# Smaller VectorE operations in the fold, and the last batch's routing gathered into one run

## The chip, the cores and the metric

One core of a Trainium2 chip runs one program. The metric is device time in microseconds (us), the median of three runs of the same kernel. The engines are TensorE (PE; its weight loads are PEld), VectorE (DVE), ScalarE (ACT), GpSimd (POOL) and SyncE (SP, which only issues DMAs here). Each takes its instructions from one queue, in order.

## The reference

The input `x` is 8 batches of 1856 rows of 256 floats. The reference takes the real part of the 2D Fourier transform of each batch and feeds the 14,848 resulting rows to a two-level mixture of experts:

```
X = fft(fft(x, axis=1), axis=2).real
group  = argmax of 4 group logits;  expert = argmax of that group's 4 expert logits
out[row] = softmax weight of group * softmax weight of expert * (relu(row @ w1[expert]) @ w2[expert])
```

There are 16 experts; `w1` is 256x1024 and `w2` is 1024x256 for each.

## The kernel before

**Phase 1** is the transform, batch by batch. `fold` (L414) adds and subtracts mirrored quarters of the batch on VectorE (`fold_rows`, `quarters`, `columns`), in place in the tiles `xq` and `BD`, and splits the result into a high and a low float16 half, `ghl` (`hi_half` on ScalarE, `lo_half` on VectorE). `s_stage` multiplies by the cosine and sine tables (matmuls `pu`, results in `U`), `leftovers` collects the odd columns in `Um`, `d_stage` does the second transform and the router's logits (matmuls `pr` and `pl`, 8 tiles for an odd batch), `rows` copies `pr` to row tiles, and `route` (L680) turns the logits into an expert, a place and a weight for each row: some twenty short VectorE steps in a chain, from the copy `lg` of `pl` to the places `posi`. It ends with 14 or 15 scatters on GpSimd that write the rows to their expert's region of a DRAM buffer, `XS`.

All work of phase 1 goes through wrappers (`self.V`, `self.A`, `self.M`, `self.Q`) that pin an instruction behind the one written just before it on its engine. Its order is written by hand: in a string such as ORDER7 each letter advances one generator by a step (F fold, S s_stage, D d_stage, L leftovers, R route, W weights, X first rows) or takes one postponed piece (s, I, i, l, d, t).

**Phase 2** is the experts. A *job* is up to four tiles of 128 rows of one expert: `layer1` (8 groups of 6 matmuls into `ph`, then ScalarE and VectorE write the halves of `hT`), and one job later `layer2` (24 matmuls into `py` for each tile, a ScalarE copy to `y`, a scatter of `y` to the output). PSUM has four buffers for `ph` (and `pu`) and two for `py` (and `pr`); `y` has four. Jobs 0, 1 and 2 take rows of which the places were settled early (after batches 4 and 6; `early_load`); jobs 3, 4 and 5 finish the same three experts and, like all that follow, need every routed row: their rows are gathered from `XS` on GpSimd with places that exist only when the last batch is routed. Then each of the other 13 experts has two jobs (4 and 3 tiles), with overflow jobs of one tile between them; job 6 is the first overflow job.

`turn_steps` (L1075) prepares a job's rows: cast to high and low halves `xh`, and a DMA transpose to `xT`. `split_steps` (L1022) prepares one expert's weights (a *unit*; units 0, 1 and 2 belong to the first three experts, unit 3 to the first overflow slot, unit 4 to the fourth expert): four square sums on ScalarE (`junk`), a small matmul, then four pairs of ScalarE and VectorE operations from the staging tile `wst` to `whl`. Units share one staging tile (overflow slots have their own).

Where instructions are not pinned (all of `layer1` and `layer2`, `turn_steps` in jobs from 2 on) a planner orders each engine's queue before the run: of the instructions that its own model of time takes as ready, the one written first. `tick` (L1288) is called after each step of a layer. It advances `weights` by about one step for each 1000 ns of planned TensorE work, the next job's row preparation by a step, and `tail`, which runs the last batch's rest, ORDER8, up to its next `|`. The routing must be complete before the first gathers are written, so `fetch(3)`, at the start of job 1, runs whatever is left of the tail. Before, ORDER8 has 30 bars: the eight ticks of job 0 write its first five products, unit 1's whole weight split comes next, and then the other products and all of the routing.

Of the kernel before, what the change touches and what calls it, by code (L numbers as in the profile page):

```python
# [14 lines left out]
ALU = mybir.AluOpType  # L15
# [23 lines left out]
WPART = 1024  # L39
LPARTS = 4  # L40
LASTZ = 7

RATE, T1, T2 = 1000, 320, 2570

# [8 lines left out]
ORDER5 = 'RsFLdFZsDlZIdsSdSZFSlFRSLLRDsDFSRRlZNZldDsdLIRSIUDLNRFSIUNRNdiDdlsUZstdDRsUZ'  # L53
ORDER6 = 'sRIDZFdISLstdSLFSssslNZiLRNZNFDRNdFRlZDSDFRSRLIdSDRRLSNUdidLsIRNRlUssDFtdRZs'
ORDER7 = 'IZWSiSZtdDLDDNLZLZZdDFldWsDdNDRDILRURRRRWSdIdRSRsRWLXSSiIZXSRlsXtUIiiURDRRsWRlSsXWXXRWWXXWSLRRWWXlWWWWWWXWWWWWWW'
ORDER8 = 'I||sisDLD|dDLi||DDsLd|||DDdL||DRRRRR||||||||dRR|IR|DRDRRRRDR|DLRLR|R||||RRdRR||d|RR|R'
BIG = 1.0e6
RS = 2.0 ** -11
E23 = 2.0 ** 23
# [206 lines left out]
class K:  # L266
# [150 lines left out]
    def fold(self, b, x, fp):  # L417

        V, sm, c32 = self.V, self.sm, self.c32
        xa, xc = x  # L420
        flat = lambda t: t.rearrange("p m e n -> p (m e n)")
        acc = sm.tile([P, 2], F32, name="acc")
        pn = self.misc[:, 480 + b:481 + b]
        ei = sm.tile([P, 1], I32, name="x_ei")
        v = sm.tile([P, NV], F32, name="x_v", bufs=4)
        sx = v[:, 0:1]
        e = sm.tile([P, NV], F32, name="x_e")
        def fold_rows(q):
            o = slice(4 * q, 4 * q + 4)
            V.tensor_tensor(out=xa[:, o], in0=xa[:, o], in1=xc[:, o], op=ALU.add)  # L430

        def squares(q):
            junk = self.cp.tile([P, 4 * 257], mybir.dt.bfloat16, name="junk", tag="junk")
            self.A.activation(junk[:, 0:4 * 257], xa[:, 4 * q:4 * q + 4].rearrange("p a d -> p (a d)"),
                              AF.Square, scale=2.0 ** 0.5, accum_out=acc[:, q:q + 1])

        def total():
            for q in range(2):
                self.M.matmul(pn, lhsT=self.one_b, rhs=top(acc)[:, q:q + 1], start=q == 0, stop=False)
            self.M.matmul(pn, lhsT=self.one_b, rhs=top(self.xa4)[:, b:b + 1], start=False, stop=True)  # L440

        def quarters(pm):
            V.tensor_tensor(out=xc[:, 4 * pm:4 * pm + 4], in0=xa[:, 0:4], in1=xa[:, 4:8],
                            op=(ALU.add, ALU.subtract)[pm])

        def columns(eo, m0, m1):
            t = xc[:, 4 * m0:4 * m1].rearrange("p (m c) d -> p m c d", c=4)
            V.tensor_tensor(out=BD[:, m0:m1, eo].rearrange("p m (c d) -> p m c d", d=128),
                            in0=t[:, :, :, eo:eo + 128], in1=t[:, :, :, 256 - eo:128 - eo:-1],
                            op=(ALU.add, ALU.subtract)[eo])  # L450

        def lo_half(part):
            V.scalar_tensor_tensor(out=part(hl[:, 1]), in0=part(BD), scalar=sx, in1=part(hl[:, 0]),
                                   op0=ALU.mult, op1=ALU.subtract)

        def hi_half(part):
            self.A.activation(part(hl[:, 0]), part(BD), AF.Copy, scale=sx)

        def exponent():
            V.tensor_scalar(out=ei, in0=pn.bitcast(I32), scalar1=24, scalar2=None,  # L460
                            op0=ALU.logical_shift_right)

        def exponents():
            V.tensor_tensor(out=e, in0=ei.broadcast_to([P, NV]), in1=c32[:, C_MUL:C_MUL + NV], op=ALU.mult)

        def powers():
            V.tensor_tensor(out=v.bitcast(I32), in0=e, in1=self.addv[:, b], op=ALU.add)

        for q in range(2):
            fold_rows(q)  # L470
            squares(q)
            yield
        if b == 0:
            BD = fp.tile([P, 2, 2, 512], F32, name="BD")
            hl = fp.tile([P, 2, 2, 2, 512], F16, name="ghl", bufs=2)
            self.fds[b] = hl, v
            total()
            quarters(0)
            columns(0, 0, 1)
            V.tensor_scalar(out=ei, in0=pn.bitcast(I32), scalar1=24, scalar2=None,  # L480
                            op0=ALU.logical_shift_right)
            V.tensor_scalar(out=sx.bitcast(I32), in0=ei, scalar1=-E23, scalar2=199 * E23, op0=ALU.mult,
                            op1=ALU.add)
            hi_half(lambda t: t[:, 0, 0])
            quarters(1)
            columns(0, 1, 2)
            hi_half(lambda t: t[:, 1, 0])
            yield
            columns(1, 0, 2)
            lo_half(lambda t: t[:, :, 0])  # L490
            yield
            hi_half(lambda t: t[:, :, 1])
            yield
            exponents()
            V.tensor_tensor(out=v[:, 1:].bitcast(I32), in0=e[:, 1:], in1=self.addv[:, b, 1:], op=ALU.add)
            lo_half(lambda t: t[:, :, 1])
            yield
            return
        total()
        yield  # L500
        for pm in range(2):
            quarters(pm)
            yield
        self.now("l")
        BD = fp.tile([P, 2, 2, 512], F32, name="BD")
        hl = fp.tile([P, 2, 2, 2, 512], F16, name="ghl", bufs=2)
        self.fds[b] = hl, v
        for eo in range(2):
            columns(eo, 0, 2)
            yield  # L510
        exponent()
        yield
        exponents()
        yield
        powers()
        yield
        hi_half(flat)
        for pm in range(1, -1, -1):
            self.later("l", lambda pm=pm: lo_half(lambda t: t[:, pm].rearrange("p e n -> p (e n)")))
        yield  # L520

    def later(self, letter, f):
# [638 lines left out]
    def phase2(self, wp):  # L1161
        tc, nc = self.tc, self.nc
        wpa = self.wpa
        with tc.tile_pool(name="h", bufs=2, reuse_waits="tile") as hp, \
# [4 lines left out]
            units, jobs = [], []  # L1169
# [5 lines left out]
            first = earliest()  # L1175
# [7 lines left out]
            o = 0  # L1183
            for e in range(len(first), NE):
# [3 lines left out]
                u = unit("s", e)  # L1188
# [14 lines left out]
            free = lambda u: -1 if before[u] is None else last[before[u]]  # L1203
            todo = sorted(range(1, len(units)), key=lambda u: (max(free(u), 0), u))
            st, ready, infos, xs = {}, {0: self.w0}, {}, {}
            state = dict(split=None, done=-1, t=0, tail=self.last_rows())

            def tail():
                if state["tail"]:
# [13 lines left out]
            def loads():  # L1223
                for u in todo:
                    if u not in st and all(pools(v)[0] != pools(u)[0] for v in st) and pools(u)[0] in pool \
                            and (units[u][0] == "s" or infos):
                        load(u)

            def weights():

                if state["split"] is None:
                    if not todo or free(todo[0]) > state["done"] or (units[todo[0]][0] == "o" and not infos):
                        return False
                    loads()
                    pn = self.misc[:, 490 + 2 * todo[0]:492 + 2 * todo[0]] if state["tail"] else self.ps.tile([P, 2], F32, name="pn", tag="misc")
                    state["split"] = self.split_steps(pool[pools(todo[0])[1]], st[todo[0]],
                                                      self.V, self.A, nc.tensor, pn, 2)
                try:
                    next(state["split"])
                except StopIteration as e:  # L1240
                    u = todo.pop(0)
                    ready[u], state["split"] = e.value, None
                    del st[u]
                    loads()
                return True
# [18 lines left out]
            def prep(n):  # L1264
                if n < len(jobs):
                    xs[n] = self.x0[n] if n < len(self.x0) else \
                        (yield from self.turn_steps(qp, *xs[n], nc.vector, nc.scalar, nc.sync))

            def tick(g, t):
                state["t"] += t  # L1270
                while state["t"] >= RATE:
                    state["t"] = state["t"] - RATE if weights() else 0
                next(g, None)
                tail()

            pend = None
            fetch(0)
# [3 lines left out]
            for n, (u, kind, slots) in enumerate(jobs):  # L1281
                while u not in ready:
                    assert weights()
                w, inv = ready[u]
                g = prep(n + 1)
                xT, wt = xs.pop(n)
                cw, toks = self.slot_weights(qp, wt, inv)
                fetch(n + 2)  # L1288
                hT = finish(self.layer1(hp, w, xT, len(slots)), lambda: tick(g, T1 * len(slots)))
                if pend:  # L1290
                    finish(self.layer2(*pend), lambda: tick(g, T2))
                    state["done"] = n - 1
                for _ in g:
                    pass
                pend = (qp, w, hT, cw, toks)
# [52 lines left out]
```

## Time and profile before

| | us |
|---|---|
| median of 3 runs (893.53 to 899.07) | 894.63 |
| the profiled execution | 889.18 |
| its span | 887.2 |
| TensorE busy in the span | 813.2 (92%) |
| VectorE, ScalarE, GpSimd busy | 531.7, 583.9, 393.9 |

Busy time is the sum of the engine's instructions in the profiled execution; a row's idle time is the gap in front of an instruction, with the event that ended it. Phase 1 lasts until about 184 us, the last batch's products and routing until about 250 us, and from there TensorE is busy in nearly all slices to the end.

### The profile page before, as it was taken

To read this page: it belongs to the slowest core of one execution; us is meant where nothing else is said; L and a number is where in the kernel's file an instruction comes from. 1 tells how busy PE (TensorE), PEld (TensorE's weight loads), DVE (VectorE), ACT (ScalarE), POOL (GpSimd) and SP (SyncE) were. 2 spreads that over 40 slices of the span, in tenths; PEclk is the share of its full clock that TensorE was granted. 3 is DMA by queue.
4 is the path that set the end of the run, shared out by engine and by line. 5 is a ranking of instruction groups with operands and counts; after the bars stand their busy time and mean duration, and the time that the engine had idled before them with its cause. 6 is when DMAs were issued, how large, how long until landed. Compare 5 with 4: busy or idle time off the path is not lost.

```text
span 887.2 us, 17624 instructions
## 1 busy us (share of the span) xinstructions
PE 813.2 (92%) x6375; PEld 580.5 (65%) x6375; DVE 531.7 (60%) x1286; ACT 583.9 (66%) x1190; POOL 393.9 (44%) x372
## 2 busy tenths in 40 slices
PE   2788989978968899799999999999999999999997
PEld 1466656635845586658686868686867777776766
DVE  6599788567625456556475665657575656566330
ACT  2576666867445477867587777768786877685331
POOL 1008777773677453515343535353443434332113
PEclk9999999979998999989999999999999999999999
DMA  9925553687287655646665758483839475632101
GB/s 348 336 96 187 193 203 116 205 239 189 70 292 197 114 166 156 181 126 169 153 177 164 194 127 225 112 264 79 273 94 235 130 206 160 175 75 52 40 19 40
DMA packets 110184, 145.86 MB, mean 164 GB/s; under 512 B 76395, under 2 KB 81799, under 8 KB 108304
## 3 DMA queue, kind: packets, MB, share of 16 engines
q1 hardware_dynamic: 92768, 99.96, 39.4%
q0 software_dynamic: 16896, 44.55, 17.0%
q8 instruction: 50, 0.82, 0.4%
q10 hardware_dynamic: 432, 0.22, 0.2%
q14 instruction: 38, 0.31, 0.1%
HBM read 97.18 MB, written 33.29 MB: 147 GB/s over the span
## 4 chain that ended last, share of the span: by engine, by line
PE 50%; issue 11%; DMA 10%; POOL 4%; DVE 3%; ACT 2%; SPq 2%; POOLq 0%; ACTq 0%; DVEq 0%
PE ph L1122 26%; PE py L1138 23%; DMA xT<-xh 6%; POOL XS L790 2%; POOL out L790 2%; DVE whl L244 2%; SPq L1091 1%; DMA wst<-w 1%; ACT whl L244 1%; DMA xg<-XS 1%; DMA xg<-XS,ii_s 1%; DMA XS<-xq,posi 1%; DVE hT L1126 0%; ACT xh L1083 0%; DMA XS<-whl,posi 0%
## 5 line engine op out<-in xcount | busy, mean ns | idle before, releaser
L1122 PE MATMUL ph<-xT,whl 128*128 128x384 f16 (+2 forms) x2112 | 368.2, 320 | 19.1 <-DVE hT L1126 8.8
L1138 PE MATMUL py<-whl,hT 128*128 128x256 f16 x2976 | 370.2, 274 | 13.8 <-ACT y L1143 11.4
L1138 PEld LDWEIGHTS <-hT 128*128 128x128 f16 x2976 | 288.1, 98 | 76.5 <-issue 13.7
L1126 DVE SCALAR_TENSOR_TENSOR hT<-ph,hT 128x128 f16<-128x128 f32 (+2 forms) x352 | 180.7, 529 | 167.2 <-ACT hT L1125 165.9
L1122 PEld LDWEIGHTS <-whl 128*128 128x128 f16 x2112 | 187.1, 99 | 137.1 <-issue 22.0
L790 POOL DMA_INDIRECT out<-y,tok x124 | 135.3, 1092 | 212.7 <-ACT y L1143 143.1
L1125 ACT ACTIVATE hT<-ph 128x128 f16<-128x128 f32 (+2 forms) x352 | 158.9, 471 | 93.3 <-PE ph L1122 90.6
L1069 POOL DMA_INDIRECT xg<-XS,ii_s x100 | 115.0, 1150 | 165.6 <-DVE hT L1126 82.8
L244 DVE SCALAR_TENSOR_TENSOR whl<-wst,e_v,whl 128x1024 f16<-128x1024 f32 x112 | 138.6, 1279 | 20.4 <-ACT whl L244 19.4
L244 ACT ACTIVATE whl<-wst,e_v 128x1024 f16<-128x1024 f32 x112 | 121.8, 1139 | 8.1 <-DVE e_v L244 7.5
L244 ACT ACTIVATE junk<-wst 128x1024 bf16<-128x1024 f32 x112 | 118.2, 1055 | 11.8 <-DMA wst<-w 11.3
L1143 ACT ACTIVATE y<-py,cws 128x256 f32<-128x256 f32 x124 | 58.6, 474 | 74.5 <-PE py L1138 58.9
L244 PE MATMUL pu<-CS,ghl 128*128 128x464 f16 (+3 forms) x384 | 84.4, 371 | 4.4 <-ACT ghl L244 4.4
L1085 DVE TENSOR_TENSOR xh<-xg,xh 128x256 f16<-128x256 f32 x116 | 48.2, 418 | 54.5 <-ACT xh L1083 54.5
L790 POOL DMA_INDIRECT XS<-whl,posi x42 | 46.8, 1115 | 73.6 <-ACT row L244 61.5
L1083 ACT CAST xh<-xg 128x256 f16<-128x256 f32 x116 | 45.1, 402 | 41.4 <-DMA xT<-xh 36.1
L244 PEld LDWEIGHTS <-ghl 128*128 128x128 f16 (+1 forms) x384 | 44.5, 119 | 36.0 <-ACT ghl L244 4.7
L790 POOL DMA_INDIRECT XS<-row,posi x45 | 51.0, 1132 | 13.9 <-issue 12.8
L244 PEld LDWEIGHTS <-U 128*128 128x128 f16 x672 | 43.1, 97 | 17.1 <-issue 9.5
L244 PE MATMUL pr<-c,U 128*128 128x256 f16 x336 | 46.4, 273 | 7.9 <-ACT whl L244 5.2
L244 DVE TENSOR_TENSOR xq<-xq 128x1028 f32<-128x1028 f32 x32 | 38.9, 1220 | 6.4 <-DMA xq<-xq 6.3
L244 ACT CAST U<-pu 128x464 f16<-128x464 f32 (+3 forms) x64 | 33.4, 549 | 12.0 <-PE pu L244 11.7
(151 smaller groups left out, 420.6 us busy)
## 6 DMA issues: line engine op xcount, KB each, us to landing
wst<-w SPq DMA_DIRECT2D x108, 512.0 KB
xq<-xq SPq DMA_DIRECT2D x14, 1028.0 KB
CS<-cs SPq DMA_DIRECT2D x8, 464.5 KB
xq<-xq SPq DMA_DIRECT2D x4, 514.0 KB
wst<-w SPq DMA_DIRECT2D x8, 256.0 KB
xT<-xh SPq DMA_TRANSPOSE x124
out<-y,tok POOLq DMA_INDIRECT x124
xg<-XS,ii_s POOLq DMA_INDIRECT x100
```

What stands on the lines that cost most here:

```text
L244: return self.tc.keep_in_program_order(f(*args, **kw))
L790: ins = self.nc.gpsimd.indirect_dma_start(out=out, out_offset=bass.IndirectOffsetOnAxis(ap=ap, axis=0), in_=in_, in_offset=None, bounds_ch ...
L1069: self.nc.gpsimd.indirect_dma_start(out=xg[:, :].bitcast(I32), out_offset=None, in_=self.XS[:, :], in_offset=bass.IndirectOffsetOnAxis(ap= ...
L1083: A.copy(xh[:, 0], xg[:, 0:D])
L1085: lo = V.tensor_tensor(out=xh[:, 1], in0=xg[:, 0:D], in1=xh[:, 0], op=ALU.subtract)
L1091: Q.dma_start(out=xT[:, :, j * P:(j + 1) * P], in_=xh, transpose=True)
L1122: nc.tensor.matmul(ph[:, 0:n * P], lhsT=w[:, wl, o:o + P], rhs=xT[:, xl * 2 + c, :], start=i == 0, stop=i == 5)
L1125: nc.scalar.activation(hT[:, f, 0], ph[:, 0:n * P], AF.Relu)
L1126: nc.vector.scalar_tensor_tensor(out=hT[:, f, 1], in0=ph[:, 0:n * P], scalar=0.0, in1=hT[:, f, 0], op0=ALU.max, op1=ALU.subtract)
L1138: nc.tensor.matmul(py, lhsT=hT[:, f, hl, j * P:(j + 1) * P], rhs=w[:, wl, 2048 + f * D:2048 + (f + 1) * D], start=i == 0, stop=i == 23)
L1143: nc.scalar.activation(y, py, AF.Copy, scale=cw)
```

## The change

1. The fold's VectorE operations of 1024 or 1028 elements a partition (`fold_rows`, `quarters`, and for batches 1 to 7 `columns` and `lo_half`) become two each, of half the size.
2. ORDER8 keeps four bars. All the products come in its first two parts, the routing in the next three, so the tail is written out by the fifth tick of job 0.
3. In `tick` the tail comes ahead of the next job's row preparation, which waits until the tail is done.
4. Row preparation of early jobs from job 2 on uses the pinned wrappers.
5. Units from 3 on are neither loaded nor split before job 3 (`LATER`, `begun`).

```diff
-ORDER8 = 'I||sisDLD|dDLi||DDsLd|||DDdL||DRRRRR||||||||dRR|IR|DRDRRRRDR|DLRLR|R||||RRdRR||d|RR|R'
+ORDER8 = 'IsisDLDdDLi|DDsLdDDDdLDDDD|dddLLLDDRRRRR|dRRRRRRRRRR|RRRRRRRRRRRRRR'
...
-            o = slice(4 * q, 4 * q + 4)
-            V.tensor_tensor(out=xa[:, o], in0=xa[:, o], in1=xc[:, o], op=ALU.add)
+            for h in range(2):
+                o = slice(4 * q + 2 * h, 4 * q + 2 * h + 2)
+                V.tensor_tensor(out=xa[:, o], in0=xa[:, o], in1=xc[:, o], op=ALU.add)
...
-            columns(eo, 0, 2)
+            for m in range(2):
+                columns(eo, m, m + 1)
...
-            self.later("l", lambda pm=pm: lo_half(lambda t: t[:, pm].rearrange("p e n -> p (e n)")))
+            def low(pm=pm):
+                for eo in range(2):
+                    lo_half(lambda t: t[:, pm, eo])
+            self.later("l", low)
...
+            begun = lambda u: u < len(first) or state["job"] >= LATER
...
-                        (yield from self.turn_steps(qp, *xs[n], nc.vector, nc.scalar, nc.sync))
+                        (yield from self.turn_steps(qp, *xs[n], *((self.V, self.A) if jobs[n][1] == "e" else
+                                                                  (nc.vector, nc.scalar)), nc.sync))
...
-                next(g, None)
                 tail()
+                if not state["tail"]:
+                    next(g, None)
```

`begun(u)` is asked both where `loads` issues a unit's load and where `weights` starts its split; `state["job"]` is set to `n` at the start of job `n`; `LATER` is 3 and `len(first)` is 3. `quarters` is halved as `fold_rows` is.

## Rows read from the trace of the kernel before

**Rows 1.** Stretches: start:end, length, busy PE PEld DVE ACT POOL, granted clock, DMA share, GB/s.
```profile
184.50:271.40 86.90, 76.04 (x543) 51.00 (x544) 45.71 (x139) 49.01 (x100) 53.20 (x52) 0.93 0.66 197
...
254.20:271.40 17.20, 10.85 (x79) 8.56 (x79) 3.13 (x14) 7.99 (x18) 13.24 (x14) 0.80 0.77 237
271.40:317.20 45.80, 38.66 (x269) 26.30 (x268) 24.56 (x67) 25.23 (x55) 24.77 (x24) 0.96 0.68 148
```

**Rows 2.** TensorE in order of time: start, us, what, count, idle before and releaser.
```profile
184.51 2.72 PE L1122 MATMUL ph<-xT,whl 128*128 128x512 f16 x6 [6.24 <-DMA xT<-xh]
...
191.32 0.82 PE L244 MATMUL pr<-c,U 128*128 128x256 f16 x6
...
211.28 0.30 PE L244 MATMUL pl<-RW,Um 128*128 128x20 f16 x6
...
215.26 5.34 PE L1122 MATMUL ph<-xT,whl 128*128 128x512 f16 x24 [3.01 <-DVE hT L1126]
...
235.37 0.19 PE L1038 MATMUL pn<-wacc,one_b 128*128 128x2 bf16 x2
...
254.24 3.22 PE L1138 MATMUL py<-whl,hT 128*128 128x256 f16 x28 [1.53 <-ACT y L1143]
263.77 5.77 PE L1138 MATMUL py<-whl,hT 128*128 128x256 f16 x30 [6.31 <-ACT y L1143]
...
271.39 4.06 PE L1122 MATMUL ph<-xT,whl 128*128 128x384 f16 x24
```

**Rows 3.** ScalarE in order of time, 202 to 262 us.
```profile
202.57 4.25 ACT L244 ACTIVATE whl<-wst,e_v 128x1024 f16<-128x1024 f32 x4
...
210.94 0.90 ACT L1083 CAST xh<-xg 128x256 f16<-128x256 f32 x2 [3.15 <-DMA xg<-XS]
...
216.85 0.49 ACT L244 COPY lg<-pl 128x280 f32<-128x280 f32 x2
...
253.71 0.47 ACT L1143 ACTIVATE y<-py,cws 128x256 f32<-128x256 f32 x1 [2.97 <-DMA out<-y,tok]
...
257.95 1.06 ACT L244 ACTIVATE junk<-wst 128x1024 bf16<-128x1024 f32 x1 [3.28 <-DMA wst<-w]
```

**Rows 4.** Scatters and gathers on GpSimd, 205 to 257 us.
```profile
206.18 0.97 POOL L790 DMA_INDIRECT XS<-xq,posi  x1 [0.31 <-issue]
...
229.15 0.97 POOL L790 DMA_INDIRECT XS<-xq,posi  x1 [0.92 <-issue]
...
249.67 0.97 POOL L790 DMA_INDIRECT XS<-xq,posi  x1 [0.30 <-issue]
...
256.06 1.05 POOL L1069 DMA_INDIRECT xg<-XS,ii_s  x1 [0.30 <-issue]
```

**Rows 5.** VectorE in order of time: unit 1's split and the last batch's places.
```profile
203.74 4.89 DVE L244 SCALAR_TENSOR_TENSOR whl<-wst,e_v,whl 128x1024 f16<-128x1024 f32 x4 [0.35 <-ACT whl L244]
...
227.02 0.56 DVE L244 TENSOR_REDUCE posi<-offp 128x15 int32<-128x240 f32 x1
```

**Rows 6.** SyncE's weight loads, 210 to 243 us.
```profile
210.72 1.79 SPq L1019 DMA_DIRECT2D wst<-w  x4
...
242.14 13.79 SPq L1019 DMA_DIRECT2D wst<-w  x8
```

**Rows 7.** Four VectorE operations of 512; all operations of the fold's last step.
```profile
214.52 2.48 DVE L1126 SCALAR_TENSOR_TENSOR hT<-ph,hT 128x512 f16<-128x512 f32 x4
...
L244 DVE TENSOR_TENSOR BD<-xq x17: 692/1218/1273, 13.3 to 150.3; 128x1024 f32<-128x1024 f32 x15, 128x512 f32<-128x512 f32 x2
```

**Rows 8.** A scatter beside a fold operation; all scatters; the wait for the first early rows.
```profile
108.00 2.38 DVE L244 TENSOR_TENSOR BD<-xq 128x1024 f32<-128x1024 f32 x2
109.26 1.96 POOL L790 DMA_INDIRECT XS<-whl,posi  x1 [0.30 <-issue]
...
L790 POOL DMA_INDIRECT XS<-row,posi x45 | 51.0, 1132 | 13.9 <-issue 12.8
...
172.95 0.40 ACT L244 CAST xh<-xg 128x256 f16<-128x256 f32 x1 [0.31 <-DMA xg<-XS]
```

More of the change, by code (lines that the diff above doesn't have):

```diff
@@ L41 @@
 LASTZ = 7
+LATER = 3
 RATE, T1, T2 = 1000, 320, 2570
@@ L55 @@
 ORDER7 = 'IZWSiSZtdDLDDNLZLZZdDFldWsDdNDRDILRURRRRWSdIdRSRsRWLXSSiIZXSRlsXtUIiiURDRRsWRlSsXWXXRWWXXWSLRRWWXlWWWWWWXWWWWWWW'
-ORDER8 = 'I||sisDLD|dDLi||DDsLd|||DDdL||DRRRRR||||||||dRR|IR|DRDRRRRDR|DLRLR|R||||RRdRR||d|RR|R'
+ORDER8 = 'IsisDLDdDLi|DDsLdDDdLDDDD|dddLLLDDRRRRR|dRRRRRRRRRR|RRRRRRRRRRRRRR'
 BIG = 1.0e6
@@ L442, in quarters @@
         def quarters(pm):
-            V.tensor_tensor(out=xc[:, 4 * pm:4 * pm + 4], in0=xa[:, 0:4], in1=xa[:, 4:8],
-                            op=(ALU.add, ALU.subtract)[pm])
+            for h in (0, 2):
+                V.tensor_tensor(out=xc[:, 4 * pm + h:4 * pm + h + 2], in0=xa[:, h:h + 2],
+                                in1=xa[:, 4 + h:6 + h], op=(ALU.add, ALU.subtract)[pm])
         def columns(eo, m0, m1):
@@ L1205, in phase2 @@
             st, ready, infos, xs = {}, {0: self.w0}, {}, {}
-            state = dict(split=None, done=-1, t=0, tail=self.last_rows())
+            state = dict(split=None, done=-1, t=0, tail=self.last_rows(), job=0)
+            begun = lambda u: u < len(first) or state["job"] >= LATER
             def tail():
@@ L1225, in loads @@
                     if u not in st and all(pools(v)[0] != pools(u)[0] for v in st) and pools(u)[0] in pool \
-                            and (units[u][0] == "s" or infos):
+                            and (units[u][0] == "s" or infos) and begun(u):
                         load(u)
@@ L1231, in weights @@
                 if state["split"] is None:
-                    if not todo or free(todo[0]) > state["done"] or (units[todo[0]][0] == "o" and not infos):
+                    if not todo or free(todo[0]) > state["done"] or (units[todo[0]][0] == "o" and not infos) \
+                            or not begun(todo[0]):
                         return False
@@ L1284, in phase2 @@
                 w, inv = ready[u]
+                state["job"] = n
                 g = prep(n + 1)
```

## The prediction

> **What bounds it now.** I read the stretches first [rows 1], then TensorE in order of time where it idles [rows 2], then each idle's releaser on its own engine [rows 3 to 6]. From 317 us on TensorE is busy in nearly every slice of the page, so time won or lost before that comes out at the end one for one. The place that the change touches lies between job 0's first matmul at 184.51 and job 3's first at 271.39. In its 86.9 us TensorE is busy 76.04 [rows 1]; the missing 10.86 are three gaps of 3.01, 1.53 and 6.31 [rows 2].
>
> Their causes differ. The first gap waits for `hT`, because ScalarE stood 3.15 us at job 2's casts: the planner had put them ahead, and their rows had not landed [rows 3]. The second waits for `y`: a `y` buffer was not free for 2.97 us, as its output scatter stood on GpSimd behind the last batch's fifteen scatters [rows 3, 4]. In the third ScalarE waits at unit 3's square sums, 3.28 us in the first, for a load that SyncE issued over 13.79 us from 242.14 on [rows 3, 6]; a finished `py` waits behind them. [...]
>
> **The change, part by part.** The sum is made against the profiled execution, 889.18 us; the median of the runs is 5.45 higher, and I add that.
>
> *Casts of job 2 pinned, behind the routing.* Four casts, four subtractions and four transposes (on SyncE) move. Their rows need batch 6's scatters, which end at 207.15 [rows 4]; pinned behind job 1's first `hT` (about 216, below) they find them landed. Gap one goes: 3.01. Job 2 starts twenty microseconds later still, so nothing new waits.
>
> *Units from 3 on wait for job 3.* Eight loads and the square sums leave the stretch. Gap three, 6.31, loses its cause, and with it the slow matmuls: 5.77 less 30 x 3.22/28 = 3.45 gives 2.3. Unit 3 is wanted by job 6 alone, over 40 us after job 3's start; its eighteen steps at about 1 us fit. Its work is covered by ScalarE's 20 us of idle in the 45.8 after 271.4 [rows 1]; without that cover it costs its four `whl` operations, 4.25 by the like row of unit 1 [rows 3]. SyncE loses its 13.79 us block, so job 3's transposes can't stand behind it.
>
> *Products and routing in one run.* Now the products run from 191.32 to 211.58 [rows 2] and the routing from the copy at 216.85 to the places at 227.58 [rows 3, 5], 10.73 us. Compact, eight products of about 1 us (0.82 and 0.31 overlapping) [rows 2] with two groups of job 0 between them end near 200; the routing, if it takes its 10.73 again, ends near 211. Batch 6 leaves GpSimd at 207.15, so the fifteen scatters run from about 211 in place of 229.15; they took 21.5 us [rows 4], so they end near 232 and not at 250.64. The gathers come 5.4 after that, near 238, and by the 15.3 us from the first gather to job 3's first matmul [rows 2, 4] rows are ready at 253. TensorE, with its gaps gone, is there at 261: they are not what is late next.
>
> What is moved past: the output scatters of job 0, some of which stood ahead of the fifteen, now queue behind them on GpSimd. Four `y` buffers hold job 0; job 1's first `y` needs one back, about 2.5 us after the fifteen end, so at 234 or 235. TensorE gets there, with its two `py` buffers full, at 231.6: job 0's second layer ends at 216 (184.5, and 2.7 for the first group, 8.3 for products, 9.6 for seven more groups, 10.9 for 96 `py`), job 1's first layer takes 10.6 (eight groups of 1.33 [rows 2]) and two tiles 5. That wait costs between nothing (if unit 2 is ready and job 2 goes first) and 6.31 plus 2.3, the like gap; by these two times it is 3, and I take 3.
>
> Unit 1's four pairs (202.57 to 208.63 [rows 3, 5]) now come behind the routing, from 211 to 218. Job 1 needs half of them, at 215; job 0's second layer, 205 to 216, hides that. Without this cover job 1 stands for up to 10. Unit 2's load is issued when unit 1 leaves the staging tile, at 218 in place of 210.72 [rows 6]. Before, unit 2 was done 31.4 after its load, at 242.1, but its small matmul stood until 235.37 [rows 2] behind the overflow lists, which follow the routing and share its PSUM bank; with the lists done by 217 about 11 of that go, and unit 2 is ready near 238, enough of it at 235, the same time as the first `y`. It is inside the 3.
>
> *Halves.* Sixty VectorE instructions more: four in batch 0, eight in each of seven. Four operations of 1024 in a row take 4.89 us [rows 5], four of 512 take 2.48 [rows 7]: behind one another halves cost nothing. Alone, one of 512 takes 692 ns where 1024 takes 1218 [rows 7], so at most 166 ns each, 10.0 in all. Below nothing: a scatter that starts inside a fold pair takes 1.96 us and ends 0.84 after the pair's end [rows 8]; if half of all the excess over 0.97 in the 45 scatters of the row went, that is 3.6. The halves are written one after the other, so the row of four is the nearest: nothing.
>
> [...]
>
> Sum: 3.01 + 1.53 + 6.31 + 2.3 - 3 = 10.15. The execution would take 879.0, the median **884.5**.
>
> **The rivals.** *The gap moves.* The fifteen scatters hold job 0's outputs longer than I think, and TensorE stands 6.31 again, with 2.3 of slow matmuls behind it, at job 1's second layer: gain 13.15 - 8.6 = 4.5, median 890. For it: GpSimd works its queue in order, and the wait is 3 already. Against it: if unit 2 is ready first, job 2's first layer can go ahead.
>
> *More goes.* From 271.4 to 317.2 TensorE idles another 7.14 [rows 1], job 3 to 5 waiting for ScalarE and transposes. With rows at 253 and unit 3 out of the way some of it can vanish: with 4 of it, 880.5; with all, 877. To this belongs a relief of GpSimd in the fold: were its chain of scatters what job 0 waits for, a start up to 3.6 earlier (873.5 with all). Against that part: the first early rows were waited for only 0.31 us [rows 8]. [...]
>
> *Ahead, but not shorter: slower.* The run stands in front of unit 1's split, and of every output. If its twenty VectorE steps still end at 227.6, each pinned behind a step of job 0, unit 1 is done at 234.7 and job 1 starts at 231, where TensorE is out of work at 216: 15, and 2.3 of slow matmuls. The scatters then end at 249 as before, the first `y` comes back at 252, and TensorE is through job 1's first layer and two tiles at 246.6: 5 and 2.3 more. Gaps one and three with their clock, 11.6, still go: 24.6 - 11.6 = 13 slower, 908. It costs from a run that ends later than 215 and passes 1% from 223 on. For it: the chain took 10.73 with VectorE busy half of the time (45.71 of 86.9 [rows 1]), so it is waiting, not work. Against it: its first part starts some fifteen microseconds earlier.
>
> *It does nothing.* The planner floats unpinned work as before (the loads are not pinned), gaps one and three come back in other places, or halves cost their 10.0 and eat the 10.15: 894.
>
> **How the numbers follow.** About 1% (8.9 us) is what a measurement of this kernel can tell. Chances: forecast 0.48, its own range 879 to 888; gap moves 0.16; more goes 0.16; nothing 0.09; slower 0.11. The range leaves out the slower case and the far end of "more": **874 to 896**. Faster (below 885.7): 0.34 of the forecast and "more": 0.50. Within 1%: the forecast's other 0.14, "gap moves" and "nothing": 0.39. Slower: 0.11.
>
> **What would show it.** In the trace after: the copy `lg` near 200 and the places near 211; the first scatter of the last batch right behind batch 6's, the last before 234; no ScalarE wait for `wst` or for early rows between 205 and 262; TensorE's idle from job 0 to job 3 under 5 us and job 3 at 259 to 264; unit 3's square sums inside job 3; fold operations in pairs of about 1.2 us. I am wrong if the places come after 220, if a gap over 5 us stands at a `py` or at job 1's or 2's first `ph`, or if phase 1 (job 0's first matmul, 184.5) moves by more than 2 either way.

## The result, and the profile after

The changed kernel takes 883.06 us (median of 4, 881.16 to 885.79); the kernel before, run beside it, 896.85 (893.53 to 900.67): a ratio of 0.990 [0.986, 0.993]. The profiled executions, 889.18 before and 883.54 after, lie only 5.64 apart, because the one of before was quicker than every timed run of it. What the traces explain is these 5.64. (The kernel that was measured has `DDsLdDDdLDDDD` as the second part of its order, one D fewer than the diff above.)

I cut both traces at the start of VectorE's first operation on `hT` in job 0 and in job 6, the 1st and the 49th of 352, and call what lies between them the transition:

| us | to job 0 | transition | from job 6 on | span |
|---|---|---|---|---|
| before | 188.2 | 134.8 | 564.3 | 887.2 |
| after | 186.3 | 127.6 | 567.9 | 881.7 |
| difference | -1.9 | -7.2 | +3.6 | -5.5 |

Stretches of the changed kernel: from job 0's first matmul to job 6, jobs 3 to 6, jobs 8 and 9 (columns as in [rows 1]):

```profile
182.56:313.80 131.24, 119.21 (x878) 82.43 (x879) 75.73 (x215) 79.98 (x165) 80.85 (x78) 0.96 0.68 186
...
266.00:332.00 66.00, 66.00 (x530) 49.21 (x529) 35.77 (x86) 45.52 (x90) 28.74 (x26) 1.00 0.47 134
...
338.60:371.20 32.60, 25.71 (x210) 19.81 (x208) 17.19 (x39) 24.25 (x46) 15.79 (x14) 0.93 0.70 193
```

and the first and the last of these in the kernel before:

```profile
184.51:323.00 138.49, 120.50 (x874) 82.63 (x875) 75.43 (x216) 80.03 (x166) 81.28 (x78) 0.94 0.66 176
...
348.00:378.60 30.60, 24.34 (x211) 19.13 (x210) 17.21 (x40) 24.11 (x46) 16.76 (x14) 0.99 0.71 210
```

Between job 0's first matmul and job 6 TensorE's idle falls from 17.99 to 12.03, and its busy time by 1.29 at a higher granted clock (0.96 against 0.94): 7.25 in all. In jobs 8 and 9 2.0 come back, of which 1.37 are busy time at a lower clock (0.93 against 0.99). But the saving does not lie where I had put it. TensorE after, against [rows 2]:

```profile
182.56 2.72 PE L1129 MATMUL ph<-xT,whl 128*128 128x512 f16 x6 [6.26 <-DMA xT<-xh]
...
185.47 1.10 PE L245 MATMUL pr<-c,U 128*128 128x256 f16 x6
...
197.44 0.30 PE L245 MATMUL pl<-RW,Um 128*128 128x20 f16 x6
...
212.53 4.48 PE L1129 MATMUL ph<-xT,whl 128*128 128x512 f16 x20
...
235.48 6.82 PE L1145 MATMUL py<-whl,hT 128*128 128x256 f16 x38 [4.89 <-ACT y L1150]
246.08 5.34 PE L1129 MATMUL ph<-xT,whl 128*128 128x512 f16 x24 [3.78 <-issue]
...
255.30 1.45 PE L1129 MATMUL ph<-xT,whl 128*128 128x512 f16 x6 [1.72 <-DVE hT L1133]
...
260.06 1.14 PE L1129 MATMUL ph<-xT,whl 128*128 128x384 f16 x6
```

Job 1 now starts without a gap, but from job 0 to job 3 TensorE still idles 11.15 us (0.29, 0.47, 4.89, 3.78 and 1.72; the first two not shown), where it was 10.86. What has gone is the idle behind job 3: from 266 to 332 TensorE is busy 66.00 of 66, where [rows 1] had 7.14 of idle between 271.4 and 317.2. (From job 3's first matmul to job 6 the idle is 0.67, where it was 7.13.)

The last batch's chain on VectorE, ScalarE and GpSimd, against [rows 3 to 5], a fence each:

```profile
208.91 0.56 DVE L245 TENSOR_REDUCE posi<-offp 128x15 int32<-128x240 f32 x1
...
212.25 1.32 DVE L245 SCALAR_TENSOR_TENSOR whl<-wst,e_v,whl 128x1024 f16<-128x1024 f32 x1
```

```profile
198.53 0.49 ACT L245 COPY lg<-pl 128x280 f32<-128x280 f32 x2
...
221.58 1.06 ACT L245 ACTIVATE junk<-wst 128x1024 bf16<-128x1024 f32 x1 [1.82 <-DMA wst<-w]
...
231.85 3.22 ACT L245 ACTIVATE whl<-wst,e_v 128x1024 f16<-128x1024 f32 x3
...
234.98 0.81 ACT L1150 ACTIVATE y<-py,cws 128x256 f32<-128x256 f32 x2
242.79 0.40 ACT L1090 CAST xh<-xg 128x256 f16<-128x256 f32 x1 [7.00 <-DMA xg<-XS,ii_s]
```

```profile
211.04 0.97 POOL L797 DMA_INDIRECT XS<-xq,posi  x1 [2.62 <-issue]
...
230.22 0.97 POOL L797 DMA_INDIRECT XS<-xq,posi  x1 [0.30 <-issue]
231.49 0.97 POOL L797 DMA_INDIRECT out<-y,tok  x1 [0.30 <-issue]
...
234.59 2.09 POOL L1076 DMA_INDIRECT xg<-XS,ii_s  x1 [0.78 <-DVE whl L245]
```

Against [rows 6], SyncE's issues: unit 2's four loads at 217.40, then the eight of units 3 and 4 among job 2's and job 3's transposes:

```profile
217.40 1.82 SPq L1026 DMA_DIRECT2D wst<-w  x4
223.54 8.15 SPq L1098 DMA_TRANSPOSE xT<-xh  x3
234.03 2.01 SPq L1026 DMA_DIRECT2D wst<-w  x4
236.73 1.53 SPq L1098 DMA_TRANSPOSE xT<-xh  x1
238.36 1.04 SPq L1026 DMA_DIRECT2D wst<-w  x2
243.69 5.55 SPq L1098 DMA_TRANSPOSE xT<-xh  x3
249.29 1.26 SPq L1026 DMA_DIRECT2D wst<-w  x2
```

The scatters' means and the fold's last step, against [rows 7, 8]:

```profile
L797 POOL DMA_INDIRECT XS<-row,posi x45 | 50.2, 1116 | 13.9 <-issue 11.6 <-ACT whl L245 0.6 <-ACT U L245 0.5
L797 POOL DMA_INDIRECT XS<-whl,posi x42 | 44.9, 1070 | 74.2 <-ACT row L245 61.9 <-issue 11.6 <-DVE m L245 0.3
...
L245 DVE TENSOR_TENSOR BD<-xq x31: 668/684/1218, 13.0 to 149.3; 128x512 f32<-128x512 f32 x30, 128x1024 f32<-128x1024 f32 x1
```

### The profile page after: what moved, and what is told of

It reads as the page before. It is cut to its first block, busy times and chain, and to the rows that moved or that the text cites. A ratio compares the mean times of both kernels' runs of the same rounds, so it can differ in the third digit from the quotient of the medians.

```text
span 881.7 us, 17685 instructions
## 1 busy us (share of the span) xinstructions
PE 814.3 (92%) x6375; PEld 581.4 (66%) x6375; DVE 536.2 (61%) x1346; ACT 583.8 (66%) x1190; POOL 390.1 (44%) x372
## 3 DMA queue, kind: packets, MB, share of 16 engines
q0 software_dynamic: 16896, 44.55, 17.9%
## 4 chain that ended last, share of the span: by engine, by line
PE 37%; issue 7%; DMA 5%; POOL 2%; ACT 1%; DVE 1%; SPq 0%; POOLq 0%; ACTq 0%
PE ph L1129 19%; PE py L1145 18%; DMA xT<-xh 5%; POOL out L797 2%; SPq L1098 0%; DVE whl L245 0%; DVE hT L1133 0%; ACT junk L245 0%; ACT xh L1090 0%; SPq L1026 0%; DVE xh L1092 0%; ACT whl L245 0%; ACT y L1150 0%; POOLq L797 0%; ACT hT L1132 0%
## 5 line engine op out<-in xcount | busy, mean ns | idle before, releaser
L1129 PEld LDWEIGHTS <-whl 128*128 128x128 f16 x2112 | 186.3, 99 | 134.1 <-issue 17.8
L797 POOL DMA_INDIRECT out<-y,tok x124 | 132.6, 1070 | 209.8 <-ACT y L1150 140.4
L1076 POOL DMA_INDIRECT xg<-XS,ii_s x100 | 117.4, 1174 | 170.5 <-DVE hT L1133 78.7
L797 POOL DMA_INDIRECT XS<-whl,posi x42 | 44.9, 1070 | 74.2 <-ACT row L245 61.9
L245 DVE TENSOR_TENSOR xq<-xq 128x514 f32<-128x514 f32 x64 | 41.1, 686 | 5.9 <-DMA xq<-xq 5.9
```

The source lines that it names most:

```text
L245: return self.tc.keep_in_program_order(f(*args, **kw))
L797: ins = self.nc.gpsimd.indirect_dma_start(out=out, out_offset=bass.IndirectOffsetOnAxis(ap=ap, axis=0), in_=in_, in_offset=None, bounds_ch ...
L1076: self.nc.gpsimd.indirect_dma_start(out=xg[:, :].bitcast(I32), out_offset=None, in_=self.XS[:, :], in_offset=bass.IndirectOffsetOnAxis(ap= ...
L1129: nc.tensor.matmul(ph[:, 0:n * P], lhsT=w[:, wl, o:o + P], rhs=xT[:, xl * 2 + c, :], start=i == 0, stop=i == 5)
```

## The experiments

They ran in four series, each on a chip of its own, and in all of them the kernel before takes 971 to 986 us at a granted clock of 0.93 to 0.95, and not 895 at 0.98; so no time below can be set beside 883.06. Every ratio is to the kernel before in the same series.

**First series.** The change in parts.

*The halves alone*, everything else as before.

```
-            V.tensor_tensor(out=xa[:, o], in0=xa[:, o], in1=xc[:, o], op=ALU.add)
+            for h in range(2):   # and so for the other four places
+                o = slice(4 * q + 2 * h, 4 * q + 2 * h + 2)
+                V.tensor_tensor(out=xa[:, o], in0=xa[:, o], in1=xc[:, o], op=ALU.add)
```

> The kernel before with the halves alone. Theory one (the chain of scatters on GpSimd bound phase 1 through the row tiles that it must free, and halves loosen it): TensorE's 5.2 us of waits at pr for the row copies shrink below 1, the mean of the 42 and 45 scatters falls from 1115 and 1132 ns to about 1070 and 1116, job 0's first hT comes 2 us earlier (186.3 against 188.2) and the time falls by 2 us, 0.2%. Rival (the earlier start of job 0 in the changed kernel is another edit's, or chance): scatters shorter all the same, job 0's first hT at 188.2 within 0.5, time the same. Rival (VectorE pays for each instruction): job 0 later by up to 5 us, time up by as much.

989.45, ratio 1.000 [0.996, 1.005].

*The order, the pinned preparation and the place of the tail in `tick`*, on the kernel before.

```
-ORDER8 = 'I||sisDLD|dDLi||DDsLd|||DDdL||...'
+ORDER8 = 'IsisDLDdDLi|DDsLdDDdLDDDD|dddLLLDDRRRRR|...'
+                        (... *((self.V, self.A) if jobs[n][1] == "e" else (nc.vector, nc.scalar)), nc.sync))
+                if not state["tail"]:
+                    next(g, None)
```

> The kernel before with the compact order of the tail, the tail ahead of row preparation, and job 2's preparation pinned; no halves, units from 3 on as before. Theory one (each of the parts removes its own gap): the 3.01 us gap at hT is gone and the last batch's scatters start near 213, but the square sums of unit 3 stand in ScalarE's queue again and wait for their load, so a gap of 5 us or more stays before job 3; the gain is 4 to 5 us (0.5%). Rival (early rows are all that counts; the later start of unit 3 changes nothing, as its loads are not pinned): no such gap, 7 us gained (0.8%).

984.92, ratio 0.999 [0.994, 1.003].

*The later loads alone.*

```
+            begun = lambda u: u < len(first) or state["job"] >= LATER
```

> The kernel before with the later start of units 3 and on, alone. Theory one: the gap of 6.31 us behind the square sums is gone or under 2, the two others stay, and 5 to 8 us are gained (0.6 to 0.9%). Rival (rows bound job 3 anyway): TensorE stands as long, now at job 3's first ph for xT, since the gathers still come at 256; the time is the same within 2 us.

985.79, ratio 0.998 [0.994, 1.002].

*The changed kernel without the later loads.*

```
-            begun = lambda u: u < len(first) or state["job"] >= LATER
```

> The changed kernel with units from 3 on started as before. Theory one: 4 to 7 us slower than the changed kernel (887 to 890), with ScalarE waiting for wst ahead of job 3. Rival (loads float in both): the same as the changed kernel within 2 us, 883 to 885.

988.5, ratio 0.996 [0.991, 1.002].

None of the four tells itself from no change. The traces show why: phase 1 takes 235 to 246 us there, the transition 156 to 164, and in both stand stretches that the first two traces don't have (below).

**Second series.** *The changed kernel again.*

```
(the changed kernel, nothing altered)
```

> The changed kernel once more, on the chip of the three kernels that follow. Every theory expects its own time of 883 us against 890 to 897 before, a ratio of 0.987 to 0.993. Where the granted clock of this chip is about 0.98, job 0's first matmul stands at 182.6 and hT of job 6 begins 9 us earlier than in the kernel before. If the 2.0 us in fold and routing are chance and not the halves, job 0's first matmul will stand at 184.5 here.

974.71, ratio 1.006 [1.003, 1.010]: slower than before by 0.6% here. The 0.987 to 0.993 that was expected is missed.

*The halves alone.*

```
(the edit of the first experiment)
```

> The halves alone: order, jobs' preparation and loads as before. Theory A (the scatters of fold and routing wait for VectorE's long operations, row tiles come free with the scatters, and TensorE waits for row tiles): the mean of XS<-whl falls from 1115 to about 1070, the wait pr <-ACT whl from 5.2 us to under 1, job 0 begins 2 us earlier, ratio 0.9965 to 0.999; the gaps of 3 to 6 us between jobs 1 and 3 remain. Theory B (the price of more instructions, my forecast's other end): job 0 begins up to 2 us later, ratio 1.000 to 1.003. Theory C (halves bring nothing, the 2.0 us are of the new order): job 0 at 184.5, ratio 1.000.

979.22, ratio 1.006 [1.002, 1.011]. Theory B's sign, at twice its size; in the first series the same kernel showed nothing.

*The changed kernel without the halves.*

```
-            for h in range(2):
-                o = slice(4 * q + 2 * h, 4 * q + 2 * h + 2)
+            o = slice(4 * q, 4 * q + 4)
```

> The changed kernel with the large VectorE operations whole, as before: the order, the pinned preparation and the later loads alone. Theory A: XS<-whl back at about 1115, job 0's first matmul at 184.5, the transition still shorter by 7 us, ratio to before 0.991 to 0.993, about 2 us above the changed kernel. Theory C: equal to the changed kernel, 0.9897. Theory D (the compact run needs the quick scatters): last scatter of the last batch after 235 and ratio above 0.995.

969.01, ratio 0.999 [0.996, 1.002].

*Loads of units 3 and 4 pinned.*

```
-                st[u] = self.load_weights(pool[pools(u)[0]], e, u == 1)
+                st[u] = self.load_weights(pool[pools(u)[0]], e, u == 1 or 3 <= u <= 4)
```

> The changed kernel with one difference: the loads of units 3 and 4 are issued at their place in the program instead of floating to where the planner put them, between job 2's transposes. Theory A (the 3.8 us gap ahead of job 2 at 246 is the fourth transpose, queued on SP behind eight weight loads): that gap falls below 1, hT of job 3 begins 2 to 4 us earlier than in the changed kernel, ratio to it 0.996 to 0.998. Theory E (job 2 waits for its gather, which shares the 16 DMA engines with the same bytes wherever the loads stand in the queue): the gap stays within 1 us of 3.8, ratio 1.000, and the squares of unit 3 wait for their weights as long or longer.

978.52, ratio 1.009 [1.006, 1.012]. It tells nothing of its question: SyncE's order in its trace is that of the changed kernel (three transposes, four loads, one, two, three, two), so the pin moved no load, and neither kernel has the gap of 3.78 here.

The three parts of the table above in this series, one profile each:

| us | to job 0 | transition | from job 6 on |
|---|---|---|---|
| halves alone | 233.0 | 165.1 | 581.8 |
| changed | 231.2 | 157.7 | 582.0 |
| changed without halves | 227.7 | 157.7 | 581.4 |

So with the order and what goes with it the transition is 7.4 shorter than with the halves alone, close to the 7.2 of the result, and taking the halves out changes nothing of it. But the kernel before has no trace in this series, and the first series, in which no kernel has the order and the later loads together, does not repeat the 7.4: the transition is 163.7 with the order alone and 160.4 and 162.4 in the two kernels without it; only the changed kernel without the later loads is shorter, 156.0. What the halves do in phase 1 these profiles don't tell: to job 0 it takes 226.4 to 233.0 with them and 227.7 without. And the wait for the first `y` of job 1's second layer belongs to the new order: it is 4.5 to 5.0 us in all eight of these twelve kernels that have the order, and 0 to 1.4 in the four that don't. TensorE's waits from 180 to 345 us in the changed kernel of this series (total, times, longest):

```profile
PE py L1145 <- issue: 15.5, 5, 11.1
...
PE py L1145 <- ACT y L1150: 5.0, 1, 5.0
```

and in the one with the halves alone, where no wait for `y` is listed:

```profile
PE py L1144 <- issue: 13.0, 9, 3.1
...
PE ph L1128 <- DMA xT<-xh: 8.4, 2, 6.0
```

**Where these series are slow.** The same 20 us of fold and routing, in the changed kernel of the result and then in that of the second series:

```profile
85.00:105.00 20.00, 18.90 (x175) 13.50 (x174) 18.60 (x50) 13.89 (x30) 15.73 (x15) 1.00 0.60 209
```

```profile
85.00:105.00 20.00, 6.70 (x37) 3.52 (x37) 4.80 (x10) 2.56 (x6) 15.27 (x15) 0.53 0.42 158
```

GpSimd sends fifteen scatters in both. TensorE does 37 matmuls in place of 175, and VectorE and ScalarE, which live on its results, stop. TensorE in order of time there:

```profile
83.41 0.27 PE L245 MATMUL pr<-c,U 128*128 128x256 f16 x1 [0.27 <-issue]
84.14 0.28 PE L245 MATMUL pr<-c,U 128*128 128x256 f16 x1 [0.46 <-issue]
84.85 0.27 PE L245 MATMUL pr<-c,U 128*128 128x256 f16 x1 [0.44 <-issue]
85.57 0.27 PE L245 MATMUL pr<-c,U 128*128 128x256 f16 x1 [0.45 <-issue]
```

One matmul in 0.71 to 0.73 us, waiting for nothing that the profile shows; in other steps it is two or three. The granted clock is still 1.00 from 80 to 85, so its fall (0.61 from 85 to 90, 0.50 from there to 110) follows the steps and does not make them. They begin 18.6 us into a run of 29 scatters without a break (64.85 to 104.54) and end about with it. Steps of 0.69 to 0.72 us from the start of one instruction of TensorE to that of the next, weight loads counted too, stand 16 to 44 times in eleven of the twelve traces. Of all 333 of them 202 lie in the second half of a run of 13 to 29 of GpSimd's indirect DMAs. In the two traces of the result, whose runs reach 101, there are 2 each, ahead of the first scatter; so a long run alone does not bring them. I tried to break the runs all the same.

**Third series.** *Pauses in the kernel before.*

```
+            if r in (6, nt - 1):
+                nc.gpsimd.memset(t[:, q, D + 2:RWID], 0.0)
```

> The kernel before, with two short pauses of GpSimd in each batch's scatters: after the seventh and the last it clears 16 padding columns of the row that it just sent, and so waits until that scatter has landed (estimate 1 to 3 us each from the 0.6 to 1.1 us between a scatter's end and its packets in the trace; 16 pauses, 16 to 48 us of GpSimd). In the runs above the kernel before took 971 to 986 us and not 895, and their traces show TensorE at one instruction per 0.70 us at the end of every unbroken run of 14 or more of GpSimd's indirect DMAs, until the run ends. Theory P (the length of the run makes it): with at most 8 in a run the slow stretches go, job 0 begins at 200 to 215 and the time is 915 to 945, a ratio of 0.93 to 0.97 where the kernel before takes 970 or more. Theory Q (TensorE is slowed by something that goes on beside the scatters, whatever GpSimd does): the slow stretches stay, ratio 1.00 to 1.03. On a chip where the kernel before takes 895 there is nothing to win and both expect 1.01 to 1.04.

960.82, ratio 0.987 [0.982, 0.992].

*The same pauses in the changed kernel.*

```
+            if r in (6, nt - 1):
+                nc.gpsimd.memset(t[:, q, D + 2:RWID], 0.0)
```

> The changed kernel with the same pauses. If theory P holds, the change is compared here without the slow stretches: the new order saves 5 to 9 us against the paused kernel before (ratio of the two 0.990 to 0.995) if the saving is of the transition, as I hold; 10 us or more if the quicker scatters of the halves count too; nothing if the pause after the last scatter takes the transition's gain away. If theory Q holds, it stands to the paused kernel before as the changed to the kernel before in the series just run, 1.006, within 0.004.

961.03, ratio 0.989 [0.982, 0.996].

The planner put the first clearing behind the last scatter as well, so the runs are 14 or 15 long, one of 29 stays in the paused kernel before (88.4 to 126.9), and only the pause between two batches is new, here in the paused changed kernel:

```profile
84.89 0.14 POOL L791 MEMSET whl<- 128x2 f32 x1
89.66 0.10 POOL L791 MEMSET whl<- 128x2 f32 x1 [4.63 <-DMA XS<-whl,posi]
```

Both stand a good 1% below the kernel before, though GpSimd waits more. That has theory P's sign; its size, 3 to 7%, it misses, and slow stretches remain inside the runs. (The steps are 27 in the paused kernel before and 9, the fewest of the twelve, in the paused changed one.) Between the two paused kernels nothing is told: 0.987 and 0.989, with intervals of about 0.006 to either side. In their profiles the transition is 157.7 and 150.7, but the first is of the longest of its kernel's five runs (978.88) and the second of the shortest of four (952.91), so these 7.0 tell nothing.

**Fourth series.** *Shorter runs.*

```
+            if r in (5, 10) and b < B - 1:
+                nc.gpsimd.memset(t[:, q - 1:q + 1, D + 2:RWID], 0.0)
```

> The changed kernel, with a pause of GpSimd ahead of the sixth and the eleventh scatter of every batch but the last (it clears the padding of the row just sent and of the next one, so it waits for the landing of the one, and the next scatter waits for it). The pauses of the two runs above fell behind the fourteenth or fifteenth scatter, of 1.4 to 5.9 us, and gained 1.1 and 1.3% where slow stretches remained; here no run in fold and routing is longer than 6. Theory P (length of an unbroken run): no stretch of 0.70 us steps before the last batch's run; GpSimd itself has 14 pauses of 1.4 to 5.9 us, 20 to 80 us, so job 0 begins at 200 to 245; time 940 to 985. Theory Q (something beside the scatters, whatever their runs): slow stretches remain inside the batches, job 0 at 230 or later, 970 to 1000. Where the kernel before takes 895 both expect 900 to 940.

979.88, ratio 0.994 [0.990, 0.999]. It did not become what was meant: the clearings fell behind the twelfth or thirteenth scatter and cost no wait, so the runs are still 13 to 15 long, and one of 29, and P and Q are not told apart:

```profile
82.16 0.17 POOL L789 MEMSET whl<- 128x4 f32 x2
82.57 0.97 POOL L799 DMA_INDIRECT XS<-whl,posi  x1 [0.24 <-POOL whl L789]
83.85 0.97 POOL L799 DMA_INDIRECT XS<-whl,posi  x1 [0.30 <-issue]
94.80 0.97 POOL L799 DMA_INDIRECT XS<-row,posi  x1 [9.98 <-ACT whl L245]
```

*Pauses without the halves.*

```
-            for h in range(2):
-                o = slice(4 * q + 2 * h, 4 * q + 2 * h + 2)
+            o = slice(4 * q, 4 * q + 4)
...
+            if r in (6, nt - 1):
+                nc.gpsimd.memset(t[:, q, D + 2:RWID], 0.0)
```

> The changed kernel without the halves, with the pause behind each batch's scatters (the changed kernel with it was at 0.989 [0.982, 0.996] of the kernel before). If the halves cost time on these chips, as the two runs 0.9989 without them and 1.0063 with them say, this is 0.980 to 0.985; if that was the length of runs and nothing of the halves, it is 0.986 to 0.992; if the halves help here as they did in the profile of the result (2.0 us), 0.990 to 0.995.

970.07, ratio 0.986 [0.976, 0.996]: it leaves all three expectations open. It is the lowest ratio of the twelve, level with the two other paused kernels. Its transition is 152.7 and that of the run above 162.4, though both have the order: single profiles differ by more than the 7.2 in question. And what pauses do where the kernel before takes 895 was not tried.

## Why the prediction was right, and where it was not

The median came out at 883.06, 1.4 below the 884.5 and inside the range. That it came so close is luck. The sum promised 10.15, and the two traces differ by 5.64: 4.5 too much. To its result I had added 5.45, the height of the median over the profiled execution in the kernel before; in the changed kernel the median lies 0.48 below it: 5.9 too much the other way. The two misses nearly cancel. Against the kernel before, run beside it, the medians are 13.8 apart, and no trace shows more of this than the 5.64. Term by term:

- **Gap one, 3.01: right.** Job 1's first layer follows at once; job 2's rows had landed when ScalarE came to them.
- **The compact run: right in time and place.** `lg` at 198.53 (said near 200), places at 208.91 to 209.47 (211), first scatter at 211.04 (211), last at 230.22 (before 234). Unit 2's load comes at 217.40 (218). Two of job 0's outputs even went ahead, at 206.03 and 207.45. The slower rival needed a run that ends after 215.
- **The new wait for job 1's first `y`: there, with 4.89 and not 3.** The mechanism was half mine: the first output behind the fifteen is issued at 231.49, so its buffer is not free before 232.5. But ScalarE had by then begun unit 2's `whl` operations, which hold it until 234.98. The 38 matmuls that follow take 6.82, where 4.37 is the pace of [rows 2] (3.22 for 28): 2.45 more at a granted clock of 0.62, behind the idle time. This is a cost that I had charged to the rival "the gap moves" alone.
- **Gap three, 6.31 and 2.3: this step failed.** The 2.3 is the slower pace of the thirty matmuls behind that gap [rows 2], at a granted clock of 0.58 from 263.77 to 269.54. "Eight loads and the square sums leave the stretch" holds for the square sums (264.53 to 270.32, inside job 3) and not for the loads. They are not pinned, and SyncE issues them from 234.03 on, earlier than the 242.14 of [rows 6]. The gathers of 234.59 meet them: their first packets start at 240.25, 5.7 after the issue, with a DMA share of 0.91 between, ScalarE waits 7.00 for its rows until 242.79, and job 2's fourth transpose goes out between two groups of loads at 236.73. The matmuls that need it begin at 246.08, 3.78 late. The run that should have moved the loads did not move them, but this trace's DMA packets show what stood in the way. On the queue that both share, the 512 packets of 4 KB of the four loads ahead start from 235.05 to 242.62, and the transpose's 512 packets of 256 bytes from 241.40, 4.7 after its issue, to 245.26; the transpose issued at 229.19, with no load in front, starts its packets at 230.37. So in this trace it waited for the loads; what a run without them there would gain was not measured. I had named this float only in the rival "it does nothing".
- **Idle under 5 from job 0 to job 3: wrong, 11.15.** Job 3's start was right all the same, 260.06 in 259 to 264, because layer 2 of job 2 is by then still to be done: 198 `py` matmuls stand ahead of it, where 288 did. That, too, is luck.
- **What I took for fixed, the 7.14 idle behind job 3, went to almost nothing.** "More goes" had it: with the rows early and unit 3's square sums inside job 3, TensorE always has a second layer to fill in (busy 66.00 of 66 from 266 on).
- **Halves at nothing, phase 1 unmoved within 2: only just right, and perhaps for a reason that I had dismissed.** VectorE is busy 4.5 us longer (531.7 to 536.2), 75 ns for each of the sixty instructions, inside my bounds of 0 and 166 and not the nothing of the sum. This repeats: 534.9 to 536.2 in all traces with the halves, 530.5 to 531.7 in those without. Yet phase 1 is 1.95 shorter. The scatters of `whl` fell from 1115 to 1070 ns, and of TensorE's waits from 20 to 182 us (18.0 in all before, 15.6 after) the one for the row tile `whl` fell from 5.2, in the first line, to 0.3, in the second:

```profile
PE pr L244 <- ACT whl L244: 5.2, 3, 2.7
```

```profile
PE pr L245 <- ACT whl L245: 0.3, 1, 0.3
```

If that is the reason, GpSimd's chain binds part of phase 1 through the row tiles that it hands back, and not through the early rows that I had looked at. The shorter scatters of `whl` repeat: without added waits their mean is 1070 to 1086 in the seven traces with the halves and 1115 to 1133 in the four without. In the three paused kernels it tells nothing (1091 with, 1063 and 1090 without), and the scatters of `row` do not part (1089 to 1117 and 1062 to 1132). In the trace before, the 24 scatters up to 155 us that start inside a `tensor_tensor` of VectorE of over 0.45 us last 1.37 us in the mean, in the trace after 1.20 (31 of them); those that start while VectorE does nothing last 0.97 in both (14 and 8). The fall of the mean of `whl` agrees with that; why such scatters last longer no run shows. The shorter wait of TensorE does not repeat: in the second series it is 3.0, 3.3 and nothing with the halves and 1.0 without, and there the halves cost 0.6%. So that the 1.95 are the halves' is not shown.
- **After job 6, 3.6 come back**, which I had not foreseen: 2.0 in jobs 8 and 9, mostly busy time at the lower clock, and 2.2 at the far end, less 0.5 between.

So "the gap moves" and "more goes" both happened and nearly cancelled, and the 5.5 of the spans are 7.2 + 1.9 - 3.6. The transition's 7.2 comes back as 7.4 in the second series, against the halves alone, and not in the first, so I hold it for likely and not for shown. Whether the whole change pays is another matter: in the second series it costs 0.6%, and without the halves it stands at 0.999.

## What to carry to other kernels

Of work that is "moved later", ask which instructions are really held there: here the unpinned loads went out from 234.03 on, among job 2's transposes, and a load that floats up can stand in the way of what is needed sooner (3.78), as the late one did (6.31). When a time agrees with a forecast, check that its terms do: here two misses of 4.5 and 5.9 made an error of 1.4. When a gap's cause goes, list what the same engine does next and price its wait with the clock behind it, not the wait alone (4.89 here, and 2.45 behind it at 0.62). And a gain of 1% that is measured on one chip is to be looked at on a second before it is believed.

## What the runs showed of the hardware

- The same kernel takes 971 to 986 us on four chips and took 895 in the series of the result. Most of the difference lies where GpSimd sends scatters and gathers in long runs: 222 to 246 us to job 0 in the twelve traces against 186 to 188, 151 to 165 in the transition against 128 to 135, 578 to 589 behind it against 564 to 568.
- In the slow stretches TensorE starts one to a few instructions in each step of about 0.71 us (37 matmuls and as many weight loads in the 20 us above). The transfers of 16 KB on an instruction queue do not seem to set the pace: across the stretch at 85 us 286 of TensorE's instructions stand between two of them in the result's trace (70.6 and 88.5) and 266 in the second series' (68.4 and 105.5), about as many in 17.9 us as in 37.1. That these transfers are TensorE's is my reading of this count alone.
- Those traces hold three tenths fewer semaphore events (9,321 against 13,376 in the changed kernel), so their releasers are to be read with care, and the recording itself may have a part in it. The cause stays open.
- A transpose that SyncE issues behind four weight loads of 512 KB starts its packets 4.7 us after its issue, when those of the loads are nearly through; with no load in front it was 1.2 us (236.73 and 229.19 in the changed kernel).
